# Third transform stage on 64x64 tiles, first stage mostly so, and a new order of all operations

## The chip, the cores and the metric

One Trainium2 chip, of which one core is used. The metric is the device time of one execution in microseconds (us). The engines are called as in the profile: PE (TensorE), PEld (its weight loads), DVE (VectorE), ACT (ScalarE), POOL (GpSimd), SP (SyncE, which here only issues DMAs).

## The reference

Two independent halves over a sequence of 2048 steps and 640 channels, joined along the channels. Half A is a diagonal complex state space model, half B a long convolution by FFT:

```python
Lam_bar = exp(dt * Lam);  B_bar = ((Lam_bar - 1) / Lam)[:, None] * Bmat
h_t = Lam_bar * h_(t-1) + B_bar @ x_t
a = 2 * Re(h @ C.T) + x * Dskip

k_shift = causal 4-tap convolution of k with shift_k      # per channel
kv = k_shift * v
y = irfft(rfft(pad(kv)) * rfft(pad(ssm_k)))[:2048] + kv * ssm_D
b = q * y
out = concat(a, b)                                       # (1, 2048, 1280), bfloat16
```

## The kernel before

The kernel records 815 operations with their footprints in SBUF, and then emits them in an order that stands in the source as a table, `ORDER`: an entry `219T2` is operation 219 on engine T (PE) with its accumulators from PSUM bank 2; A is ACT, V is DVE, G is POOL, S is SP. Each engine runs its entries strictly in the table's order; semaphores between engines follow from the footprints. So the table sets which engine empties which PSUM group, which PSUM banks a group waits for, and the order of the DMAs on SP. A small letter `t` says that a PE operation is issued *narrow*, on smaller tiles of the array.

Half A: `ld_x`, `ld_B` (L512, L517, L547) load, `up2`, `up1`, `up0` (matmuls L581 and L602, evictions L598, L622, L648) build sums over 2, 4, 8 and 16 steps, `coarse` scans over blocks of 16 (`cs_...`, L679 to L690), `dn3` to `dn0` with their additions `ad3` to `ad0` (matmuls L225 and L229, additions L728 on DVE; on ACT, L726, the addition is a second matmul by the identity and a copy) bring the states back down, and the sixteen `C` products (matmuls L225 or L229, eviction `ev_C`, L754) project them, with `xd` (L737, x times D, which waits for `ld_Dr`) added. `gC` (L571, L575) scales the C matrix. The factors come from `dt`, `rn` (Exp on ACT, L383 and L388), `al_s` (Sin, L414), a chain of small DVE steps (`pv`, `dtf`, `rho` ... `fi`), POOL (`fn1`, `ph`) and four expansions `rr` (L457).

Half B, in two halves of 320 channels (0 and 1): the taps of the short convolution, `cm` on ACT (L206) or DVE (L205) and their sums `ca` (L840) and product with v `cx` (L841), per block d of 128 channels; there is one buffer for k, so `ld_k` of block d+1 (L814) waits for the last tap of block d (`cm0_0` for block 1). `pl` writes a finished block to DRAM (L847), the relay `rl` reads it back in another layout (L857). Then the transforms: `s1h`, `s1k` (matmuls L876 wide, L881 narrow, eviction `e1`, L886), `s2` (L900, eviction `e2`, L913), the products `pp`, `pq`, `py`, `pz` (L924 to L931), `r2`, the third stage (L951 wide, L948 narrow, eviction `er2`, L956), `r1` (L972, eviction `er1`, L988 or L990), `em1` (L995), and stores. Tables of sines for these come from POOL (`wqh` L309, `gqh` L350) and ACT (`w_s` L314, `g_s` L354, `i_s` L325, `f1_s` L289), and for the scan `sph` (L472), `sin`, `cos` (L477, L478).

`P.narrow` holds the operations that stand in the table with a small t; in `s1` and `r2` it chooses between two forms.

Of the kernel before, what the change touches and what calls it, by code (L numbers as in the profile page):

```python
# [1097 lines left out]
def plain_order(P):  # L1098
# [16 lines left out]


ORDER = (
# [40 lines left out]
)  # L1158


# [68 lines left out]
```

## Time and profile before

| | us |
|---|---|
| median of 3 runs (188.85 to 190.1) | 190.03 |
| span of the profiled execution | 187.3 |
| busy: PE, PEld | 175.6, 126.3 |
| busy: DVE, ACT, POOL | 158.0, 147.7, 72.6 |

The page gives no time of the profiled execution beside its span; the median lies 2.7 us above it. Granted TensorE clock: 0.999 over the span. Busy time is the union of an engine's instructions; an engine that is idle beside another that sets the pace costs nothing. In the tables by line, `out<-in` are the program's tiles: nearly all lie in one big SBUF buffer, `arena`, and all accumulators in `acc`.

### The profile page before, as it was taken

To read this page: it belongs to the slowest core of one execution; us is meant where nothing else is said; L and a number is where in the kernel's file an instruction comes from. 1 tells how busy PE (TensorE), PEld (TensorE's weight loads), DVE (VectorE), ACT (ScalarE), POOL (GpSimd) and SP (SyncE) were. 2 spreads that over 40 slices of the span, in tenths; PEclk is the share of its full clock that TensorE was granted. 3 is DMA by queue.
4 is the path that set the end of the run, shared out by engine and by line. 5 is a ranking of instruction groups with operands and counts; after the bars stand their busy time and mean duration, and the time that the engine had idled before them with its cause. 6 is when DMAs were issued, how large, how long until landed. Compare 5 with 4: busy or idle time off the path is not lost.

```text
span 187.3 us, 7665 instructions
## 1 busy us (share of the span) xinstructions
PE 175.6 (94%) x3398; PEld 126.3 (67%) x3399; DVE 158.0 (84%) x225; ACT 147.7 (79%) x181; POOL 72.6 (39%) x68
## 2 busy tenths in 40 slices
PE   7998999999799979979997999999999999999992
PEld 2565666677468756656685688776588876887770
DVE  3537964679959899999969999899999999998961
ACT  2469699989899979999997997997898883985000
POOL 8679999900000000008803925730740000551620
PEclk9999999999999999999999999999999999999999
DMA  5999999799999989999989479402496993058996
GB/s 153 191 184 158 200 143 140 141 174 182 198 253 154 290 179 152 180 182 154 138 109 251 154 170 133 75 5 72 122 196 120 210 227 85 15 160 187 208 219 173
DMA packets 106682, 30.15 MB, mean 161 GB/s; under 512 B 101274, under 2 KB 106010, under 8 KB 106650
## 3 DMA queue, kind: packets, MB, share of 16 engines
q1 hardware_dynamic: 106332, 29.35, 86.7%
q8 instruction: 26, 0.43, 1.1%
q10 hardware_dynamic: 318, 0.33, 0.6%
q14 instruction: 6, 0.05, 0.1%
HBM read 11.32 MB, written 7.86 MB: 102 GB/s over the span
## 4 chain that ended last, share of the span: by engine, by line
PE 54%; DVE 23%; DMA 9%; ACT 8%; issue 3%; DVEq 0%; ACTq 0%
PE acc L225 17%; PE acc L581 13%; DMA arena<-in_B_k_dram 9%; PE acc L229 6%; DVE arena L728 6%; PE acc L900 6%; DVE arena L205 5%; ACT arena L913 5%; PE acc L951 4%; DVE arena L840 3%; PE acc L972 3%; PE acc L539 2%; DVE arena L754 2%; PE acc L881 1%; ACT arena L886 1%
## 5 line engine op out<-in xcount | busy, mean ns | idle before, releaser
L581 PE MATMUL acc<-arena 128*64 128x512 bf16 x400 | 45.6, 380 | 1.8 <-DVE arena L457 1.1
L913 ACT CAST arena<-acc 128x960 bf16<-128x960 f32 (+1 forms) x43 | 37.4, 916 | 4.0 <-PE acc L900 2.2
L225 PE MATMUL acc<-arena 128*128 128x320 bf16 (+2 forms) x255 | 36.4, 297 | 2.2 <-DVE arena L754 1.1
L581 PEld LDWEIGHTS <-arena 128*64 128x64 bf16 x400 | 26.0, 110 | 17.8 <-DVE arena L457 1.3
L886 ACT CAST arena<-acc 128x1024 bf16<-128x1024 f32 x37 | 35.8, 1034 | 2.1 <-PE acc L881 2.0
L225 PEld LDWEIGHTS <-arena 128*128 128x128 bf16 x256 | 23.7, 98 | 12.1 <-DVE arena L754 1.3
L841 POOL TENSOR_TENSOR arena<-arena 128x2048 bf16<-128x2048 bf16 x2 | 8.8, 4410 | 53.7 <-DVE arena L840 46.1
L900 PE MATMUL acc<-arena 128*64 128x160 bf16 x512 | 23.6, 235 | 1.8 <-DVE arena L679 1.4
L900 PEld LDWEIGHTS <-arena 128*64 128x64 bf16 x512 | 18.6, 110 | 8.3 <-ACT arena L913 2.2
L229 PE MATMUL acc<-arena 128*64 128x320 bf16 (+3 forms) x258 | 23.2, 313 | 0.5 <-DVE arena L690 0.5
L840 DVE TENSOR_TENSOR arena<-arena 128x2048 bf16<-128x2048 bf16 x14 | 17.6, 1256 | 4.5 <-ACT arena L206 4.3
L728 DVE TENSOR_TENSOR arena<-acc,arena 128x1024 bf16<-128x1024 f32 (+2 forms) x19 | 20.4, 1114 | 0.9 <-PE acc L229 0.5
L760 POOL TENSOR_TENSOR arena<-arena 128x640 bf16<-128x640 f32 x3 | 4.2, 1416 | 32.6 <-ACT arena L752 32.6
L956 ACT CAST arena<-acc 128x1024 bf16<-128x1024 f32 x16 | 15.4, 1025 | 1.7 <-PE acc L951 1.6
L229 PEld LDWEIGHTS <-arena 128*64 128x64 bf16 x258 | 13.0, 110 | 3.5 <-DVE arena L690 0.6
L876 PE MATMUL acc<-arena 128*64 128x128 bf16 x400 | 14.6, 220 | 0.2 <-ACT arena L886 0.2
L876 PEld LDWEIGHTS <-arena 128*64 128x64 bf16 x400 | 12.9, 110 | 2.4 <-ACT arena L886 0.9
L205 DVE TENSOR_SCALAR arena<-arena 128x2048 bf16<-128x2048 bf16 x15 | 11.0, 749 | 3.6 <-DMA arena<-in_B_k_dram 3.5
L754 DVE TENSOR_TENSOR arena<-acc,arena 128x640 bf16<-128x640 f32 x13 | 10.7, 820 | 3.5 <-PE acc L225 2.2
L206 ACT ACTIVATE arena<-arena 128x2048 bf16<-128x2048 bf16 (+2 forms) x10 | 11.1, 1112 | 1.5 <-DMA arena<-in_B_k_dram 1.5
L924 DVE TENSOR_TENSOR arena<-arena 128x2560 bf16<-128x2560 bf16 x8 | 11.9, 1484 | 0.1
L602 PE MATMUL acc<-arena 128*64 128x256 bf16 (+2 forms) x140 | 11.6, 291 | 0.1
(142 smaller groups left out, 284.4 us busy)
## 6 DMA issues: line engine op xcount, KB each, us to landing
out_dram<-arena SPq DMA_DIRECT2D x32, 160.0 KB, 3.3
arena<-in_B_ssm_k_dram SPq DMA_DIRECT2D x8, 320.0 KB, 6.1
kv_rows<-arena SPq DMA_DIRECT2D x5, 512.0 KB, 4.7
arena<-kv_rows SPq DMA_DIRECT2D x16, 160.0 KB, 4.0
arena<-in_A_x_dram SPq DMA_DIRECT2D x16, 160.0 KB, 3.5
arena<-in_B_q_dram SPq DMA_DIRECT2D x8, 320.0 KB, 6.3
arena<-in_A_B_im_dram ACTq DMA_DIRECT2D x1, 160.0 KB, 2.8
arena<-in_A_B_re_dram SPq DMA_DIRECT2D x1, 160.0 KB, 3.0
```

What stands on the lines that cost most here:

```text
L205: vm = lambda e: lambda out, in_, by: e.tensor_scalar_mul(out=out, in0=in_, scalar1=by)
L225: e.matmul(out, lhsT=lhsT, rhs=rhs, start=start, stop=stop, skip_group_check=True)
L229: e.matmul(out[half], lhsT=lhsT[:, half], rhs=rhs, start=start, stop=stop, skip_group_check=True, tile_position=(0, 64 * r))
L581: e.matmul(o[64 * r:64 * r + 64], lhsT=self.BT[j][:, r, d, :], rhs=self.XP[:, d, 2 * q:2 * q + 2], start=(d == 0), stop=(d == 4), skip_gro ...
L728: e.tensor_tensor(out=o, in0=b, in1=o, op=ALU.add)
L754: e.tensor_tensor(out=two(ys), in0=two(B)[:, :, 0:320], in1=two(ys), op=ALU.add)
L840: P.add(f"ca{d}_{j}", tt, lambda e: e.tensor_tensor(out=t1, in0=t1, in1=t2, op=ALU.add), outs=[t1], ins=[t1, t2])
L876: e.matmul(B[64 * b:64 * b + 64, 128 * i:128 * i + 128], lhsT=lh[i], rhs=F[:, b, :], start=True, stop=True, tile_position=(0, 64 * b))
L886: P.add(f"e1{what}{hf}_{u}", {PACT: act(1024), PDVE: dve(1024)}, lambda e, B: c.CP[e](out=out, in_=(B.rearrange("p (l n s k) -> p k s l n" ...
L900: e.matmul(B[64 * s:64 * s + 64, 512 * b + 160 * i:512 * b + 160 * i + 160], lhsT=c.W[:, k, 64 * b:64 * b + 64], rhs=self.AS[hf][:, k, 160 ...
L913: c.CP[e](out=out, in_=b.rearrange("p r (k j n) -> p r k j n", k=n, j=4) if nj > 1 else b.rearrange("p r (k x) -> p r k x", k=n))
L956: P.add(f"er2{hf}_{u}", {PACT: act(1024), PDVE: dve(1024)}, lambda e, B: c.CP[e](out=out, in_=B.rearrange("p (s n b) -> p b s n", s=2, n=4 ...
```

## The change

Only the table `ORDER` differs. It issues 18 of the 20 `r2` operations narrow (before: none) and 34 of the 40 `s1` operations (before: 15), moves about 70 evictions and small operations between engines, and puts all operations in a new order. POOL runs 65 instead of 64 operations. Two of the 46 old and 44 new lines of the table:

```diff
-    "168A0 156G0 161S0 0V0 58G0 6T0 17G0 167A0 162S0 110G0 19V0 147G0 87V0 11G0 18V0 89A0 90S0 12G0 3T1 42G0 13V0 88S0 182S0 "
+    "0V0 161A0 30G0 167S0 7T0 26G0 17G0 168A0 162S0 58G0 20V0 110G0 21V0 122V0 112G0 8T1 19V0 87V0 46G0 125V0 23V0 89A0 28V0 36V0 "
...
-    "557T2 564A4 684T0 789G0 558V2 559V0 678T6 685A0 680T4 679V6 783G0 790S0 690T2 681A4 682T0 691V2 686T6 556G0 784S0 683A0 "
+    "787T0 672V0 780V0 673V0 782A4 777V0 783G0 557T2 788A0 778S0 688t6 558V2 686t4 689A6 694t0 565G0 687V4 559G0 692t2 695A0 560T6 "
```

In a narrow `s1` each of eight groups is 4 matmuls of 64x64 by 64 columns, which leave out the zero half of a block diagonal factor, instead of 2 matmuls of 128x64 by 128 columns. In a narrow `r2` each 64x128 by 128 matmul is two of 64x64.

What the new table does on single engines, at three places. First ACT at the start of the program, ahead of its first evictions of `up2` (L598); `js0` is L206 128x64, `f1_s` L289, `dt` L383, the copies of the turned B matrix L526. Before:

```order
L383 ACT_TABLE_LOAD
L383 ACTIVATE arena<-arena 128x10
L526 COPY arena<-acc 128x640 x3
L388 ACTIVATE arena<-arena 128x10 x3
L526 COPY arena<-acc 128x640
L598 CAST arena<-acc 128x2x2x256
L388 ACTIVATE arena<-arena 128x10 x2
L414 ACT_TABLE_LOAD
L414 ACTIVATE arena<-arena 128x80
```

And now, at the same place:

```order
L206 ACT_TABLE_LOAD
L206 ACTIVATE arena<-arena 128x64
L289 ACT_TABLE_LOAD
L289 ACTIVATE arena<-arena 128x64
L383 ACT_TABLE_LOAD
L383 ACTIVATE arena<-arena 128x10
L388 ACTIVATE arena<-arena 128x10
L526 COPY arena<-acc 128x640 x2
L388 ACTIVATE arena<-arena 128x10
L526 COPY arena<-acc 128x640
L388 ACTIVATE arena<-arena 128x10
L354 ACT_TABLE_LOAD
```

`js0` and `f1_s` moved ahead of `dt`, one `rn` moved ahead of the first copies, and three loads of the activation table stand where there was one.

Second, the stretch that follows on ACT, now up to the first tap of block 0 (L206 128x2048) and `sin` (L477); `rn` is L388, `al_s` L414, `sw` L796:

```order
L796 CAST arena<-arena 128x20
L388 ACT_TABLE_LOAD
L388 ACTIVATE arena<-arena 128x10
L414 ACT_TABLE_LOAD
L414 ACTIVATE arena<-arena 128x80
L598 CAST arena<-acc 128x2x2x256
L354 ACTIVATE arena<-arena 128x32x32 x2
L388 ACT_TABLE_LOAD
L388 ACTIVATE arena<-arena 128x10
L598 CAST arena<-acc 128x2x2x256
L314 ACT_TABLE_LOAD
L314 ACTIVATE arena<-arena 128x1024
```

Two of the five `rn` moved in among the sines, each with a load ahead of it and one behind it; before, nothing but the load ahead of `al_s` stood there.

Third, DVE after the scan's last step (L690), up to the additions of the level below. Before:

```order
L690 TENSOR_TENSOR arena<-arena 128x5x128
L840 TENSOR_TENSOR arena<-arena 128x2048
L728 TENSOR_TENSOR arena<-acc,arena 128x5x128
L886 CAST arena<-acc 128x64x2x8
L728 TENSOR_TENSOR arena<-acc,arena 128x4x256
L728 TENSOR_TENSOR arena<-acc,arena 128x256 x2
L575 CAST arena<-acc 128x2x320
L205 TENSOR_SCALAR arena<-arena 128x2048 x2
L728 TENSOR_TENSOR arena<-acc,arena 128x4x256
L728 TENSOR_TENSOR arena<-acc,arena 128x2x2x256 x2
L913 CAST arena<-acc 128x2x3x160
L205 TENSOR_SCALAR arena<-arena 128x2048
```

And now:

```order
L690 TENSOR_TENSOR arena<-arena 128x5x128
L728 TENSOR_TENSOR arena<-acc,arena 128x4x256
L728 TENSOR_TENSOR arena<-acc,arena 128x5x128
L886 CAST arena<-acc 128x64x2x8 x2
L728 TENSOR_TENSOR arena<-acc,arena 128x256
L205 TENSOR_SCALAR arena<-arena 128x2048
L728 TENSOR_TENSOR arena<-acc,arena 128x256
L205 TENSOR_SCALAR arena<-arena 128x2048
L728 TENSOR_TENSOR arena<-acc,arena 128x4x256
L913 CAST arena<-acc 128x2x3x160 x2
L728 TENSOR_TENSOR arena<-acc,arena 128x2x2x256
L205 TENSOR_SCALAR arena<-arena 128x2048
```

The evictions of gC (L575) and one of the two 1024-wide additions left DVE for ACT; one more e1k (L886) and one more e2k (L913) came.

74 rows, old and new, of the table ORDER are left out of this document.

## The prediction

> **What bounds the kernel now.** First the page: three engines are nearly full, and the average does not say which of them sets the end.
>
> ```profile
> PE 175.6 (94%) x3398; PEld 126.3 (67%) x3399; DVE 158.0 (84%) x225; ACT 147.7 (79%) x181; POOL 72.6 (39%) x68
> ```
>
> So I cut the span at DVE instructions that I know by name: the landing of the second k block (41.15), of the fourth (65.20), `ev_C0` (98.5), `ev_C4` (127.9), `er10_16` (161.8) and the last eviction (184.4). The view of busy time by stretch then reads (length, PE, PEld, DVE, ACT, POOL):
>
> ```profile
> 41.15:65.20 24.05, 22.81 (x373) 16.52 (x369) 21.18 (x27) 22.60 (x34) 0.00 (x0) 1.00 1.12 214
> 65.20:98.50 33.30, 29.98 (x743) 21.56 (x740) 31.48 (x41) 31.78 (x40) 8.14 (x2) 1.00 1.05 157
> 98.50:127.90 29.40, 28.15 (x650) 21.38 (x653) 28.11 (x29) 26.27 (x30) 15.30 (x6) 1.00 0.59 125
> 127.90:161.80 33.90, 33.29 (x791) 25.31 (x781) 32.79 (x41) 27.33 (x33) 5.62 (x4) 1.00 0.73 143
> 161.80:184.40 22.60, 21.80 (x516) 17.08 (x514) 18.96 (x22) 8.34 (x9) 9.50 (x6) 1.00 0.74 181
> ```
>
> DVE idles 2.9, 1.8, 1.3 and 1.1 us in the first four, out of 120.7. From the landing of k1 to 161.8 DVE is the bound, and ACT beside it up to 98.5. PE's 90 to 98% hides its own waits, because the modelled ends of matmuls overlap. Only the last stretch, four C products and the end of r1, is PE's: DVE idles 3.6 us there. Where DVE does idle before that, the timeline names transposing loads:
>
> ```profile
> 41.15 1.42 DVE L205 TENSOR_SCALAR arena<-arena 128x2048 bf16<-128x2048 bf16 x2 [0.90 <-DMA arena<-in_B_k_dram]
> 53.96 0.75 DVE L205 TENSOR_SCALAR arena<-arena 128x2048 bf16<-128x2048 bf16 x1 [1.90 <-DMA arena<-in_B_k_dram]
> 65.20 1.42 DVE L205 TENSOR_SCALAR arena<-arena 128x2048 bf16<-128x2048 bf16 x2 [0.65 <-DMA arena<-in_B_k_dram]
> 97.87 0.49 DVE L737 TENSOR_TENSOR arena<-arena 128x640 bf16<-128x640 bf16 x1 [1.38 <-DMA arena<-in_A_Dskip_dram]
> ```
>
> Thus the time is: when k1 lands, plus DVE's work from there, plus DVE's waits, plus PE's tail.
>
> **PE's part of the change, costed at nothing.** The rows of a wide s1, a narrow s1, r1, a wide r2, and a change of tile shape:
>
> ```profile
> 122.93 1.55 PE L876 MATMUL acc<-arena 128*64 128x128 bf16 x48 [0.16 <-ACT arena L886]
> 97.40 1.00 PE L881 MATMUL acc<-arena 64*64 64x64 bf16 x96
> 153.27 1.63 PE L972 MATMUL acc<-arena 64*64 64x80 bf16 x160
> 161.65 5.50 PE L951 MATMUL acc<-arena 64*128 64x128 bf16 x160
> 108.20 0.61 PE L900 MATMUL acc<-arena 128*64 128x160 bf16 x12
> 108.73 0.75 PE L881 MATMUL acc<-arena 64*64 64x64 bf16 x64
> 112.39 2.79 PE acc L900 x72
> 105.64 0.62 PE L229 MATMUL acc<-arena 128*64 128x512 bf16 x4
> 106.10 0.61 PE L876 MATMUL acc<-arena 128*64 128x128 bf16 x16
> ```
>
> A wide s1 takes 1.55/3 = 0.52 us, a narrow one 1.00/3 = 0.33; narrow goes from 15 to 34 operations: -19 x 0.19 = -3.6 us. No trace row shows a narrow r2 (32 matmuls on 64x64 tiles, 128 columns). By r1, 10.2 ns for 80 columns, it is 16.3 ns per matmul and 0.52 us, against 5.50/10 = 0.55 wide. If r1's pace held whatever the width, it would be 0.33; if splitting in two doubled it, 1.1. I take 0.52, the nearest row: -18 x 0.03 = -0.5. Changes of tile shape rise from 52 to 65; the twelve matmuls at 108.20 hold PE 0.53 us ahead of one, against 2.79/6 = 0.46 in a row (the chain's 72): 13 x 0.07 = +0.9. Three more additions on ACT (`ad1_0`, `ad1_6`, `ad0_9`; `ad3_0` leaves) double their matmuls by identity ones, 0.46 each from 105.64 to 106.10, less 0.3: +1.0. Net: -2.2 us. DVE covers it: in the r2 stage ACT and DVE empty PSUM at one operation per 1/(1/1.025 + 1/1.218) = 0.56 us, which is already the 0.55 that PE shows.
>
> ```profile
> L956 ACT CAST arena<-acc 128x1024 bf16<-128x1024 f32 x16 | 15.4, 1025 | 1.7 <-PE acc L951 1.6
> L956 DVE CAST arena<-acc 128x1024 bf16<-128x1024 f32 x4 | 4.7, 1218 | 0.0
> ```
>
> Without that cover a narrow r2 at 1.1 would lengthen r2 by 18 x 0.55 = 10 us; the s1 rows speak against that, since there the split made an operation shorter, so I exclude it and keep up to +1.5.
>
> **Term 1, k1 lands later: +3.7 us.** The new order mixes Exp and Sin on ACT, and so the program has eight table loads where it had two.
>
> ```profile
> 2.29 1.28 ACT L383 ACT_TABLE_LOAD   x1 [2.29 <-DVE arena L258]
> 6.56 0.21 ACT L383 ACTIVATE arena<-arena 128x10 bf16<-128x10 f32 x1 [3.00 <-DVE arena L378]
> 7.92 1.29 ACT L526 COPY arena<-acc 128x640 bf16<-128x640 bf16 x2 [0.56 <-PE acc L524]
> 12.82 1.28 ACT L414 ACT_TABLE_LOAD   x1
> 14.11 0.27 ACT L414 ACTIVATE arena<-arena 128x80 f32<-128x80 int32 x1
> 30.30 2.00 ACT L206 ACTIVATE arena<-arena 128x2048 bf16<-128x2048 bf16 x1
> 10.38 0.22 POOL L406 COPY arena<-arena 128x10 int32<-128x10 int32 x1 [2.68 <-DVE arena L300]
> 12.83 0.32 POOL L410 TENSOR_TENSOR arena<-arena 128x80 int32<-128x80 int32 x1
> 8.25 0.16 DVE L385 TENSOR_TENSOR arena<-arena 128x10 f32<-128x10 f32 x1
> 29.80 5.08 SPq L814 DMA_TRANSPOSE arena<-in_B_v_dram  x1
> 34.99 2.69 SPq L814 DMA_TRANSPOSE arena<-in_B_k_dram  x1
> ```
>
> Now: the load before `dt` sits behind `js0` and `f1_s`, which wait for DVE and have loads of their own; I estimate `dt` at 7.2 instead of 6.56. `rn` waits for `rho` (8.25 + 0.65), and both `ev_B0` now stand behind it: done at 10.4 instead of 9.2 at the latest (the copies at 7.92 end), so PE's first `up2` starts about 1.2 us later, which also hides that `ld_sk` and `ld_D` now stand ahead of three x loads on SP. `fn1` on POOL comes at 11.0, `ph` ends 5.0 us of POOL work later at 16.0 (13.15 now). ACT needs a load for `g_s` (which waits for `gqh`, 13.3), one for `rn`, one for `al_s`: 13.3 + 1.13 + 0.35 + 1.28 + 0.2 + 1.28 + 0.27 = 17.8 against 14.38. From there to the end of `cm0_0` stand 17.9 us of work in the new order (four taps at 2.0, three evictions at 1.0, three `g_s` at 1.15, three `w_s` at 1.06, `sin` 1.27, the rest 1.0; starts overlap by 0.1 each) and two more loads, 2.6: 38.3, or 39 if `sin` waits for `sph` on POOL. Now it ends at 32.30, and `ld_k1`, which overwrites the only k buffer, is issued at 34.99 because `ld_v0` held SP. Then it is issued at 38.7: +3.7. At the low end ACT's 7.3 idle us before 14 swallow all but the two late loads, and k1 is 0.5 late; at the high end POOL's waits make it 5.
>
> [...]
>
> **Term 2, DVE from k1 to k3's taps: +0.7.** There `cx0`, `e1h0_0`, `ev_up21_4`, three up0 evictions and the first two steps of the coarse scan enter (8.2 us), two `rr`, `gm` and small ones leave (4.9). The 3.3 us first fill the waits of 1.90 and 0.65.
>
> **Term 3, DVE from k3's taps to `ev_C0`: -3.4.**
>
> ```profile
> L886 DVE CAST arena<-acc 128x1024 bf16<-128x1024 f32 x3 | 3.6, 1215 | 0.0
> L913 DVE CAST arena<-acc 128x960 bf16<-128x960 f32 x3 | 3.5, 1154 | 0.0
> L575 DVE CAST arena<-acc 128x640 bf16<-128x640 f32 x4 | 3.3, 815 | 0.0
> L728 DVE TENSOR_TENSOR arena<-acc,arena 128x1024 bf16<-128x1024 f32 x16 | 18.8, 1217 | 0.9 <-PE acc L229 0.5
> ```
>
> Four gC evictions leave (3.3), with `e1k0_1`, `ad1_0`, `e2k0_8` (3.6), `xd0`, an up0b eviction and the two scan steps (2.2): 9.1. `ad3_0`, two e1k and two e2k enter (5.6).
>
> **Term 4, the wait for D: -1.4.** `xd0` goes to POOL and `ld_Dr` stands ahead of `ld_v3` and `ld_k4` on SP instead of behind them and the four loads of h1.
>
> **Term 5, ACT and the relay behind it: +1.8.** SP now issues a `ld_C1` ahead of `pl2`, and another inside the relay:
>
> ```profile
> 70.90 1.79 SPq L556 DMA_TRANSPOSE arena<-in_A_C_im_dram  x1
> 78.98 1.03 ACT L886 CAST arena<-acc 128x1024 bf16<-128x1024 f32 x1
> 96.80 2.04 ACT L206 ACTIVATE arena<-arena 128x2048 bf16<-128x2048 bf16 x1
> ```
>
> So the first half of the relay is complete 3.4 us later than k1's shift alone says, at about 81, which leaves PE's first s1k at 81.3 (77.1 now, with 3 us of slack), and its eviction at 82 (78.98). From there to `cm4_0` ACT has 20 instructions of 17 us, as now (17.8): the last of s2k is out at 97.6, `C0` ends at 99.8, `ev_C0` runs at 99.9. By terms 1 to 4 alone DVE would be there at 98.1: +1.8. The bounds are 0 (the relay lands in time) and 3.5.
>
> **Term 6, DVE after that: +0.2.** To `er10_16` DVE's instructions sum to 64.7 us instead of 64.4 by their rows; `xd1` (0.5) leaves right behind `ev_C0`, the rest grows. **Term 7, the tail: +0.4.** One r1 of 0.43 us moves behind `r10_16`; the last C products stay PE-bound.
>
> Sum: 3.7 + 0.7 - 3.4 - 1.4 + 1.8 + 0.2 + 0.4 = +2.0 us. The profiled span of 187.3 becomes 189.3; the median of the runs, 190.03, lies 2.7 above the span, so **192.0**.
>
> **Rivals.** *PE was the bound after all, or ACT hides its loads* (0.2); the page's chain speaks for it:
>
> ```profile
> PE 54%; DVE 23%; DMA 9%; ACT 8%; issue 3%; DVEq 0%; ACTq 0%
> ```
>
>  In this case terms 1 and 5 are near zero and 0.7 - 3.4 - 1.4 + 0.2 + 0.4 = -3.5 remains: 186.5. It decides where `cm0_0` still ends before 35, when `ld_v0` leaves SP. *The delay is absorbed* (0.2): ACT catches up before C0, term 5 is 0: 190.2. *The whole delay arrives* (0.15): PE's s1k waits for the relay and DVE runs dry there, so term 3 saves nothing: 195.4. The forecast itself has 0.45, from 190.5 to 194.
>
> The range takes the terms' bounds: 186 to 196. One per cent, about what a measurement of this kernel can tell from no change, is 1.9 us. Faster holds the first rival, 0.2; slower the third and 0.6 of the forecast, 0.42; within 0.38.
>
> **What would show it.** Eight table loads of 1.28 us; `ld_k1` on SP near 38.7 and k1's taps on DVE near 44.9; no wait of DVE for D; s1k's first eviction near 82; `ev_C0` near 99.9; r21's ten operations still at 0.55 us each; s1 narrow at 0.33. I am wrong if k1 lands before 42, or if DVE is no longer full between 65 and 160.

## The result, and the profile after

The changed kernel takes **207.5 us** (median of 4, 206.76 to 208.19) against 189.4 for the kernel before on the same chip: ratio 1.099, 95% interval 1.091 to 1.108. The forecast was 192.0 with a range of 186 to 196, so the sign was right and the time was missed by 15.5 us. Losses below are given as ratios to the kernel before, measured beside each run; the ratios leave out slow executions, more than 1.5% above the fastest of their kernel, which the medians keep. 1% is 1.9 us.

The page of the changed kernel, with the lines that answer to the one shown of before and two more: the clock that TensorE was granted (all nines before), and the queue `q8` of instructions, whose packets are compared with TensorE's program further below.

```profile
PE 187.8 (91%) x4066; PEld 132.7 (65%) x4066; DVE 162.4 (79%) x229; ACT 151.2 (74%) x181; POOL 75.1 (37%) x69
...
PEclk9999999799999999975999999999999999999999
...
q8 instruction: 32, 0.52, 1.2%
```

Every engine is busier in us and less busy as a share, and the clock has two dips, near 36 and near 92 us. TensorE has 668 more matmuls; before, `q8` had carried

```profile
q8 instruction: 26, 0.43, 1.1%
```

That is six packets more; the prediction does not count them. Here is the span of the changed kernel cut at the same instructions (first tap of k1, first tap of k3, `ev_C0`, `ev_C4`, `er10_16`, last eviction), in the columns of the prediction:

```profile
43.66:70.50 26.84, 26.84 (x580) 18.56 (x580) 24.87 (x31) 23.62 (x34) 2.33 (x1) 1.00 1.11 197
70.50:106.48 35.98, 30.00 (x695) 19.93 (x691) 31.31 (x35) 30.06 (x41) 10.91 (x4) 0.91 1.09 173
106.48:140.02 33.54, 32.27 (x900) 23.38 (x902) 31.56 (x33) 29.36 (x31) 14.86 (x6) 1.00 0.60 115
140.02:173.46 33.44, 33.00 (x772) 26.61 (x770) 29.16 (x35) 23.05 (x28) 9.16 (x5) 1.00 0.56 108
173.46:202.46 29.00, 27.24 (x784) 23.34 (x784) 18.56 (x23) 7.81 (x9) 4.00 (x3) 1.00 0.59 147
```

The stretches were 24.05, 33.30, 29.40, 33.90 and 22.60 us long. So 2.5 us are lost before k1's taps, then 2.8, 2.7, 3.7 in the next two together (`ev_C4` now runs 2.8 us behind the end of its product, so the cut between them has moved), and 6.4 in the tail. DVE, called the bound, idles 4.7 us in the second row and 4.3 us in the fourth; it no longer decides there. Three places hold most of the loss.

**The table loads.** Eight, 1.28 us each; from the timeline of ACT (start, us, line):

```profile
2.62 1.28 ACT L206 ACT_TABLE_LOAD   x1 [2.62 <-DVE arena L263]
...
14.10 1.28 ACT L388 ACT_TABLE_LOAD   x1
15.62 1.28 ACT L414 ACT_TABLE_LOAD   x1
20.38 1.28 ACT L388 ACT_TABLE_LOAD   x1
22.80 1.28 ACT L314 ACT_TABLE_LOAD   x1
```

```profile
38.65 2.30 SPq L814 DMA_TRANSPOSE arena<-in_B_k_dram  x1
```

`ld_k1` is issued at 38.65, where the prediction had 38.7. Behind these loads an eviction of `up2` on ACT comes late, and TensorE waits for it once, up to 35.27; the clock is halved from 35.44 for 3.4 us, which is the dip near 36. From the waits, and busy time with the clock (third from the end):

```profile
PE acc L581 <- ACT arena L598: 2.2, 1, 2.2
35.00:40.00 5.00, 4.72 (x28) 2.18 (x30) 5.00 (x5) 4.38 (x5) 2.48 (x2) 0.66 0.40 85
```

**A stop of TensorE up to 91.87, and half the clock from within it.** Busy time in stretches of 5 us, the two rows in question, and from the timeline the row that begins when the stop ends, with ACT's next row:

```profile
85.00:90.00 5.00, 2.83 (x135) 2.18 (x128) 4.97 (x6) 4.08 (x6) 3.28 (x2) 1.00 1.04 210
90.00:95.00 5.00, 3.13 (x74) 1.74 (x73) 2.25 (x4) 1.36 (x2) 2.17 (x1) 0.51 1.09 139
```

```profile
91.87 0.64 PE L881 MATMUL acc<-arena 64*64 64x64 bf16 x32 [2.37 <-issue]
...
94.40 1.01 ACT L726 CAST arena<-acc 128x1024 bf16<-128x1024 f32 x1 [3.64 <-PE acc L229]
```

"Issue" says that TensorE waited for nothing that the profile shows. The granted clock is 0.51 from 90 to 95 us (halved from 90.05 for 6.8 us), and ACT and DVE run dry there (1.36 and 2.25 us busy of 5). `ev_C0` comes at 106.48 instead of the 99.9 forecast.

**A third stage of twice the length.** The groups of r2's lines, narrow (L948) and its evictions on ACT:

```profile
L956 ACT CAST arena<-acc 128x1024 bf16<-128x1024 f32 x17 | 16.7, 1019 | 8.5 <-PE acc L948 8.4
L948 PE MATMUL acc<-arena 64*64 64x128 bf16 x576 | 18.7, 282 | 0.2 <-issue 0.2
L948 PEld LDWEIGHTS <-arena 64*64 64x64 bf16 x576 | 17.9, 213 | 0.8 <-issue 0.6
```

A narrow r2 starts 0.96 to 1.01 us after the one before it, where the two stand in a row and no stop lies between, and a wide one takes 0.55; and ACT idles 8.4 us waiting for it (1.6 before).

### The profile page after: what moved, and what is told of

Read it like the earlier page. It is cut to its first block, busy times and chain, and to the rows that moved or that the text cites. A ratio compares the mean times of both kernels' runs of the same rounds, so it can differ in the third digit from the quotient of the medians.

```text
span 205.5 us, 8999 instructions
## 1 busy us (share of the span) xinstructions
PE 187.8 (91%) x4066; PEld 132.7 (65%) x4066; DVE 162.4 (79%) x229; ACT 151.2 (74%) x181; POOL 75.1 (37%) x69
## 4 chain that ended last, share of the span: by engine, by line
PE 59%; ACT 20%; DVE 11%; POOL 4%; issue 4%; ACTq 0%; DVEq 0%; POOLq 0%
PE acc L229 14%; PE acc L225 12%; PE acc L581 11%; PE acc L948 9%; ACT arena L913 5%; DVE arena L728 5%; PE acc L881 4%; PE acc L900 4%; PE acc L602 3%; ACT arena L206 3%; ACT arena L575 2%; PE acc L972 2%; POOL arena L350 2%; DVE arena L754 1%; DVE arena L886 1%
## 5 line engine op out<-in xcount | busy, mean ns | idle before, releaser
L581 PEld LDWEIGHTS <-arena 128*64 128x64 bf16 x400 | 24.6, 113 | 22.6 <-ACT arena L598 2.7
L886 ACT CAST arena<-acc 128x1024 bf16<-128x1024 f32 x36 | 35.0, 1034 | 4.0 <-PE acc L881 2.9
L913 ACT CAST arena<-acc 128x960 bf16<-128x960 f32 (+1 forms) x39 | 34.1, 904 | 5.1 <-PE acc L900 2.9
L229 PE MATMUL acc<-arena 128*64 128x320 bf16 (+3 forms) x406 | 34.6, 320 | 0.5
L225 PE MATMUL acc<-arena 128*128 128x320 bf16 (+3 forms) x183 | 27.7, 302 | 2.1 <-DVE arena L690 1.4
L229 PEld LDWEIGHTS <-arena 128*64 128x64 bf16 x406 | 22.1, 113 | 7.5 <-issue 1.4
L225 PEld LDWEIGHTS <-arena 128*128 128x128 bf16 x183 | 16.6, 98 | 9.4 <-ACT arena L886 2.1
L900 PEld LDWEIGHTS <-arena 128*64 128x64 bf16 x512 | 19.0, 110 | 4.5 <-ACT arena L913 2.5
L948 PE MATMUL acc<-arena 64*64 64x128 bf16 x576 | 18.7, 282 | 0.2 <-issue 0.2
L737 POOL TENSOR_TENSOR arena<-arena 128x640 bf16<-128x640 bf16 x5 | 7.0, 1397 | 31.7 <-DMA arena<-in_A_Dskip_dram 29.9
L948 PEld LDWEIGHTS <-arena 64*64 64x64 bf16 x576 | 17.9, 213 | 0.8 <-issue 0.6
L881 PEld LDWEIGHTS <-arena 64*64 64x64 bf16 x1088 | 11.4, 110 | 10.0 <-issue 6.6
L881 PE MATMUL acc<-arena 64*64 64x64 bf16 x1088 | 13.9, 197 | 3.4 <-issue 2.9
L598 DVE CAST arena<-acc 128x1024 bf16<-128x1024 f32 x7 | 8.5, 1219 | 7.3 <-ACT arena L414 6.1
L205 DVE TENSOR_SCALAR arena<-arena 128x2048 bf16<-128x2048 bf16 (+1 forms) x16 | 12.2, 773 | 1.5 <-DMA arena<-in_B_k_dram 1.3
```

Of the source, the lines that this page charges most:

```text
L225: e.matmul(out, lhsT=lhsT, rhs=rhs, start=start, stop=stop, skip_group_check=True)
L229: e.matmul(out[half], lhsT=lhsT[:, half], rhs=rhs, start=start, stop=stop, skip_group_check=True, tile_position=(0, 64 * r))
L581: e.matmul(o[64 * r:64 * r + 64], lhsT=self.BT[j][:, r, d, :], rhs=self.XP[:, d, 2 * q:2 * q + 2], start=(d == 0), stop=(d == 4), skip_gro ...
L881: e.matmul(B[64 * b:64 * b + 64, 512 * l + 64 * i:512 * l + 64 * i + 64], lhsT=lh[i][ps], rhs=F[ps, b, 64 * l:64 * l + 64], start=True, st ...
L886: P.add(f"e1{what}{hf}_{u}", {PACT: act(1024), PDVE: dve(1024)}, lambda e, B: c.CP[e](out=out, in_=(B.rearrange("p (l n s k) -> p k s l n" ...
L900: e.matmul(B[64 * s:64 * s + 64, 512 * b + 160 * i:512 * b + 160 * i + 160], lhsT=c.W[:, k, 64 * b:64 * b + 64], rhs=self.AS[hf][:, k, 160 ...
```

## The experiments

In `ORDER` an entry is a number, an engine letter and a bank; a small `t` makes an operation narrow.

### The third stage

Wide again in the changed kernel (e1), and narrow in the kernel before (e2):

```diff
- ... 678t0 ... 696t2 ... 680t6 ...      (18 entries)
+ ... 678T0 ... 696T2 ... 680T6 ...
```

> The changed kernel with the tile split of the third stage (r2) taken back in its 18 operations; order and everything else as changed. Theory A (a narrow r2 costs 1.0 us of TensorE against 0.5 wide, because each of its 32 pairs of weight load and matmul takes as long as one of the 16 wide pairs): the r21 stage from r10_16 to C8 shrinks from 11.3 to 6 us, the eight narrow r20 operations save up to another 4, total 197 to 202 us. Rival B (the pace of r2 is set by ScalarE's evictions or by the new order): r2 operations stay near 1.0 us apart, total 205 to 208.

> The kernel before with the 18 r2 operations of the change as 64x64 tiles and nothing else changed. Theory A: 1.0 us an operation, 9 us more at most, 195 to 199 us. Rival B: 189 to 191 us.

Measured: e1 200.7 us, ratio 1.062 (1.048 to 1.076) instead of 1.099; e2 197.6 us, ratio 1.050 (1.041 to 1.059). Theory A holds: the tile split of r2 costs 5% by itself and 3.7% within the change, and rival B is out. It does not say why a pair of load and matmul takes 30 ns. Weights of a wide and of a narrow r2 are columns of Y that lie 80 bytes apart, so e7, in the kernel before, takes them from a matrix whose elements stand side by side (the third stage's output is then left out):

```diff
-  e.matmul(B[ms, ...], lhsT=lh[i][s][r][:, ms], rhs=rh, ...)
+  e.matmul(B[ms, ...], lhsT=c.W[64 * s:64 * s + 64, 2 * i + r, ms], rhs=rh, ...)
```

> The kernel before with the 18 r2 operations as 64x64 tiles, but with their weights read from the constant matrix W, 64 elements side by side, in place of columns of Y that lie 80 bytes apart; so the third stage's output is left out. Theory H (the weight load of a narrow tile is slow because its columns lie apart): r2 at 0.3 to 0.6 us an operation, weight load near 110 ns, total 187 to 191 us. Rival I (a 64x64 tile with 128 moving columns takes 30 ns a pair whatever its weights): 0.95 to 1.0 us an operation, total 195 to 199 us.

The weight loads of e2, the groups of e7, and two rows of e7's timeline in the r21 stage:

```profile
L948 PEld LDWEIGHTS <-arena 64*64 64x64 bf16 x576 | 17.7, 212 | 0.8 <-ACT arena L752 0.3 <-issue 0.3
```

```profile
L948 PE MATMUL acc<-arena 64*64 64x128 bf16 x576 | 10.1, 218 | 4.0 <-issue 4.0
L948 PEld LDWEIGHTS <-arena 64*64 64x64 bf16 x576 | 8.6, 107 | 5.3 <-issue 4.9
```

```profile
164.67 1.98 PE L948 MATMUL acc<-arena 64*64 64x128 bf16 x128 [1.15 <-issue]
168.40 0.92 PE L948 MATMUL acc<-arena 64*64 64x128 bf16 x51 [1.74 <-issue]
```

The weight load falls from 212 ns in e2 to 107, and operations start 0.44 to 0.57 us apart where no stop lies between: theory H for the pace. (e7 changes the tensor that the weights come from together with their spacing.) The total, 192.9 us in one run, is above H's 187 to 191; TensorE now stops for 4.0 us of "issue" in these operations. The faster narrow operations run into stops of the kind that is taken up below.

### Table loads, and the order without narrow operations

e3 brings two `rn` forward and puts `f1_s` and `js0` behind the last `rn` on ACT; two loads are left:

```diff
- 15A0 (js0) ... 34A0 (f1_s) ... 94A0 ... 98A0 ... 99A0 ... 100A0 ... 97A0 ... 101A0
+ 94A0 ... 98A0 ... 99A0 ... 100A0 97A0 101A0 34A0 15A0
```

> The changed kernel with four small operations of ScalarE's prologue moved (two rn brought forward, f1_s and js0 put behind the last rn), so that its exponentials stand together and two table loads of 1.28 us are left of eight. Theory C (the delay of 4 us to VectorE's chain arrives at the end): k1's load issued near 35, C0 ended 4 us earlier, total 202 to 204 us. Rival D (the delay is swallowed by the stall of TensorE between 85 and 100 us, which has a cause of its own, the last part of the relay): total 205.5 to 208 us.

> The changed kernel with the changed order kept, but the third stage wide in all 20 operations and the first stage narrow only in the 15 operations that are narrow before. Theory F (TensorE's program arrives in packets of 256 instructions, one packet ahead; narrow operations use them up twice as fast, and TensorE stands still when a packet is late): the stall of 2.4 us ahead of s1k0_9 and the half clock after it go, total 193 to 197 us against 200.7 with 34 narrow. Rival G (the stall is the wait for the relay's last part, whatever the tiles): stall and half clock stay, total 199 to 202 us.

> As e5_order_only, and the four small ScalarE operations moved so that two table loads are left of eight. Theory C (the delay of VectorE's chain arrives): 3 to 4 us less than e5_order_only, 190 to 193 us. Rival D (swallowed): within 1 us of e5_order_only.

e3: ratio 1.080 (1.067 to 1.094), 204.6 us by the median and 202.5 by the ratio: theory C's 202 to 204 and not D's 205.5 to 208. `ld_k1` comes at 36.92, not near 35, and the stop ahead of `s1k0_9` grows to 3.16 us. e5: 198.8 us, ratio 1.060 (1.053 to 1.067). Its stop at 91.87 and the half clock there are gone, as theory F has it, but the total misses F's 193 to 197: it has another stop of 1.56 us at `s1h1_6`, and lies nearer to G's 199 to 202. Against e1 (1.062) the 19 narrow operations of s1 thus cost nothing that can be told in this order. e6: 194.7 us, ratio 1.036 (1.028 to 1.045): the six loads cost 4.1 us against e5, and nearly all of it arrives, from `cm0_0` (37.20 to 33.30) to the last C product (4.4 us). Theory C, where no larger stop hides it. Its 190 to 193 was 2 us too low with e5's. A part of the 4.1 us is not the loads' own time: e5 has half the clock from 34.9 for 3.4 us, after a wait of 2.5 us for ACT, and e6 has neither. In the changed kernel twenty matmuls take 4.04 us at that place, in e12 (below), which has all eight loads but no half clock there, 2.35.

e11 asks for the start of the order, where `ev_B0` waits on ACT behind the first `rn`:

```diff
- 98A0 (rn) ... 166A0 ... 164A5 (the two ev_B0)
+ 166A0 ... 164A5 98A0
```

> As e6_order_two_loads (changed order, narrow set of before, two table loads), and the first rn put behind the two ev_B0 that it stood ahead of on ScalarE. Theory K (the order's own cost begins with up2, which starts 1.8 us later because ev_B0 waits behind rn for VectorE's rho): ev_B0 ends near 8.8 us, up2 starts 1.3 us or more earlier, and 1 to 1.5 us of it arrives: 193 to 194 us against 194.7. Rival L (it is absorbed, since ScalarE's evictions and not TensorE's start set the pace): 194.2 to 195.2 us.

194.5 us, ratio 1.037 (1.026 to 1.048). `ev_B0` ends at 8.16 instead of 10.40, and `up20_4` still starts at 19.66 (19.42 in e6), because it then waits 0.94 us for a load of B. So the traces show rival L, absorbed; the interval alone would not tell 1 us.

### TensorE's program

s1 narrow in the kernel before, in the 34 operations of the change (with two that were narrow already and are not among them, 36):

```diff
- ... 201T4 ... 195T6 ... 191T2 ... 203T0 ...      (21 entries)
+ ... 201t4 ... 195t6 ... 191t2 ... 203t0 ...
```

> The kernel before with the first stage narrow in the 34 operations of the change (15 before) and nothing else changed. If TensorE's time there is hidden by the evictions, as the prediction has it: 188.5 to 190 us. If it counts: 19 operations by 0.2 to 0.25 us, 185 to 187 us.

Both were wrong: 194.1 us, ratio 1.035 (1.027 to 1.043), **slower**, although each narrow s1 does run in 0.27 us. Its page has 336 more matmuls and TensorE stops five times for 0.5 to 1.7 us of "issue".

What these stops have in common is their place in the program. The trace's DMA records have queue `q8` in packets of 16,384 bytes (32 in the changed kernel; 32 times 256 are 8,192, and TensorE has 8,170 records). Here are TensorE's records (weight loads, matmuls, semaphore waits) counted up to each stop over 0.5 us that waits for nothing shown:

```
kernel   operation, stop in us, records ahead of it, modulo 256
after    s1k0_9 2.37: 194    r11_6 0.73: 194
e1       s1k0_9 2.37: 192    r10_28 0.87: 193    r11_22 2.08: 192
e2       C14 1.34: 194
e4       s1k0_8 0.90: 193    s2k0_0 0.54: 194    s1k1_5 0.88: 193    r21_6 0.68: 193    r11_16 1.68: 194
e5       s1h1_6 1.56: 195    C10 0.80: 194
e7       r20_1 0.68: 195     r10_0 0.96: 195     r21_2 1.15: 194     r21_5 1.74: 194    C14 1.13: 195
```

All lie between 192 and 195 of 256, as do 17 more in e3, e6, e8 to e12, e15 and e18; some traces lack one or two records, which moves the count. `q8` has 29 packets in e4, with 672 instructions more than before, and 27 in e17 (below), with 256 more, against 26 before. So a packet is read here as 256 instructions of TensorE. A packet begins when TensorE has about entered the one ahead of it (median lag 1.0 us after, 1.1 before, at most 4.4 and 3.4), takes 0.9 to 1.8 us, and TensorE, where it stood, goes on some 1.2 to 1.7 us after its end (for `s1k0_9` the packet ends at 90.39 and TensorE goes on at 91.87). So by estimate a packet's worth of instructions that is used up in less than about 3.8 us makes TensorE stand, where the next packet has the usual lag; it is no fixed bound, for in the changed kernel four packets used up in 3.3 to 3.6 us (up to 52.3, 113.8, 130.4 and 133.8) brought no stop over 0.3 us. The packet for `s1k0_9` began 4.36 us after that point. Theory F: a narrow operation has twice the instructions of a wide one (64 against 32 in s1 and r2, weight loads included), and where it is also quick (s1: 0.27 us against 0.52) it runs the program dry.

To test it, e8 and e9 add 64 matmuls (128 instructions) to the warm-up in about the same time, so that all boundaries fall half a packet further on (e8 in the operations shown, e9 in `warm` 5, 2, 3 and 8):

```diff
-            for _ in range(2):
-                e.matmul(B[:, 0:512], ...)
+            n, w = (18, 56) if k in (6, 7, 0, 1) else (2, 512)
+            for _ in range(n):
+                e.matmul(B[:, 0:w], ...)
```

> The changed kernel with 64 more matmuls, so 128 more instructions, in the warm-up: four of its operations do 18 matmuls of 56 columns in place of 2 of 512, about the same time. Every later instruction then stands half a packet further on. Theory F (packets of 256): every stop of TensorE that waits for nothing shown again begins at the same count within a packet (192 of 256), so at other operations than before: no stop of 2.4 us ahead of s1k0_9, one of 1 to 3 us two narrow operations earlier if that packet is as late. Rival G (relay): the stop stays ahead of s1k0_9. The total is not what tells them apart: 203 to 209 us.

> The kernel before with 64 more matmuls in the warm-up, as in e8_shift_packets (128 more instructions in about the same time), nothing else. Theory F (packets of 256 instructions, a stop when one is late): the boundaries fall half a packet further on, at operations where they did not fall before; if the kernel before owes its time to boundaries that fall well, stops of 0.5 to 2 us appear at a count of 192 within a packet and the total is 189 to 193 us. Rival J (packets hardly matter where first and third stage are mostly wide): no stop, total within 1 us of the kernel before.

e8 (206.1 us in one run): no stop ahead of `s1k0_9`, and one of 1.60 us ahead of `s1k0_8`, two operations later rather than earlier, as far into its packet (194). Rival G, the relay, is out. e9 is the run that matters: with the work of the kernel before unchanged, 194.2 us, **ratio 1.033 (1.023 to 1.043)**. Its timeline has stops that the kernel before has not (records modulo 256: 193, 192, 193):

```profile
156.34 0.58 PE L973 MATMUL acc<-arena 64*64 64x80 bf16 x42 [1.42 <-issue]
166.52 2.82 PE L952 MATMUL acc<-arena 64*128 64x128 bf16 x83 [0.52 <-issue]
176.03 0.61 PE L973 MATMUL acc<-arena 64*64 64x80 bf16 x23 [2.36 <-issue]
```

> The kernel before with 112 more matmuls in the warm-up, 224 more instructions: almost a whole packet, so the boundaries fall nearly where they fell. Theory F, from the profile of before: packets used up in under 3.8 us cost 5.4 us at 128 more instructions (measured 6.3) and 1.4 us at 224: 188.5 to 190.5 us. Rival N (the extra matmuls themselves cost the time of e9_before_shift): more of them, 195 us or above.

> The kernel before with 128 more matmuls in the warm-up, 256 more instructions: one whole packet, so from the warm-up on every boundary falls where it fell. Theory F: no stop, the time of the kernel before, 187 to 189.5 us (one packet more to fetch, early, where nothing waits). Rival N (the extra matmuls cost the time): 194 us or above.

These add 112 and 128 matmuls in the same way. e15: ratio 1.013 (1.006 to 1.019), 190 us as F had it. e17, exactly one packet: **ratio 1.003 (0.998 to 1.008)**, and the longest wait of this kind in its list of waits is 0.4 us:

```profile
PE acc L882 <- issue: 0.4, 1, 0.4
```

Half a packet costs 6.3 us, seven eighths 2.4, a whole one nothing. Rivals J and N are out: it is the place of the boundaries, and the kernel before has them where they cost nothing.

The same in the changed kernel (32 more instructions), in its order with two loads (208 more), and in the kernel before with s1 wide, as it is and with 220 more:

> The changed kernel with 16 more matmuls, 32 more instructions, in the warm-up. Theory F, from its profile: packets used up in under 3.8 us cost 5.1 us as it stands and 1.4 us at 32 more: 203 to 205 us. Rival J: 206.5 to 208.5 us.

> As e6_order_two_loads (changed order, narrow set of before, two table loads) with 104 more matmuls, 208 more instructions, in the warm-up. Theory F, from the profile of e6: packets used up in under 3.8 us cost 2.9 us as it stands and 0.5 us with the boundaries 208 further on: 191 to 192.5 us; what is left against the kernel before is the order's own. Rival J: 194 to 195.5 us.

> The kernel before with the first stage wide in all 40 operations, so 15 of them go from 0.27 to 0.52 us of TensorE and 480 instructions go. Theory F: two packets fewer, no stops, but up to 15 x 0.25 = 3.7 us more of TensorE, of which evictions hide a part: 187 to 191 us. If narrow operations of the first stage pay for themselves in the kernel before: 190 to 192 us; if their packets cost as much as they save: 187 to 189 us.

> The kernel before with the first stage wide (e10_before_s1_wide) and 110 more matmuls in the warm-up (13 of 78 columns in each of its ten operations in place of 2 of 512): 220 more instructions. Theory F, worked out from the profile of e10: with the boundaries of the packets 220 instructions further on no packet is used up in less than 3.8 us, so the stop of 2.3 us ahead of C10 and the half clock after it go; e10 was 2.4 us ahead of the kernel before until C9, total 185 to 187 us. Rival J (boundaries don't decide; e10's stop is of another kind): 191 to 193 us.

e16: 204.0 us, ratio 1.087 (1.082 to 1.092), within F's 203 to 205: 1.2% less by the ratios for 32 instructions more. Its stop in s1k is gone, but the clock is still halved from 89.94 for 3.4 us (6.8 in the changed kernel), after TensorE waited 1.46 us for DVE up to 88.10; e8 has the same from 90.37. e14: 193.1 us, ratio 1.029 (1.024 to 1.034); no stop is left, yet half a microsecond above F's range. e10: 192.0 us, ratio 1.024 (1.017 to 1.032), above F's 187 to 191, which had no stop; it was 2.3 us ahead of the kernel before at C9 and lost it and more at one boundary:

```profile
155.77 6.47 PE L225 MATMUL acc<-arena 128*128 128x320 bf16 x34 [2.30 <-issue]
```

e13 takes that stop away and comes to 189.9 us, ratio 1.012 (1.007 to 1.017): better than e10, but its 2.3 us ahead are gone (a wait of 2.05 us of `s2h0_27` for DVE, which e10 has not, ends at 67.97), so 185 to 187 was wrong and it does not beat the kernel before.

Why a packet begins late: e12 leaves out two transposing loads.

```diff
+  None if f"{n}{d}" in ("v3", "k4") else e.dma_start_transpose(...)
```

> The changed kernel with two transposing loads left out (ld_v3 and ld_k4, issued between 81 and 88 us), so that the taps of the fourth and fifth block work on old data. Theory F (the packet for s1k0_9 is late, 4.4 us from its request to its beginning, because the core's DMA queues are full of these transfers): the packet begins within 2 us of its request, the stop ahead of s1k0_9 is below 0.5 us and the clock stays at full speed from 90 to 97 us. Rival M (the packet is late for a reason in TensorE's own sequencer): the stop stays above 1.5 us. The total also gains from the waits that the two loads took with them, so it is not what tells them apart.

205.2 us in one run. The packet for `s1k0_9` begins 2.04 us after TensorE went on into the packet ahead of it, 3.88 in the changed kernel. But TensorE had just stood 1.47 us at that boundary (0.29 in the changed kernel), because the packet ahead began later (2.8 us behind its own point against 1.3); from the beginning of that stop it is 3.5 against 4.2 us. The stop ahead of `s1k0_9` is still 2.06 us, M's number (here the view puts it down to DVE, L886), and the clock is still halved, from 91.77 for 3.4 us. So this run does not show that other transfers make the packets late; what sets the lag is open.

Last, the changed kernel with its causes taken away together: r2 wide, two loads, 108 more instructions.

> The changed kernel with the third stage wide, two table loads (as e3_two_loads) and 54 more matmuls, 108 more instructions, in the warm-up; the order and the 34 narrow operations of the first stage are kept. From e1's profile packets used up in under 3.8 us cost 5.4 us there and 1.0 us with boundaries 112 further on. Theory F: 200.7 - 4.1 (loads) - 2 to 4.4 = 192 to 194.5 us. Rival J (the place of the boundaries doesn't matter with 34 narrow operations): 196 to 197.5 us.

198.4 us, ratio 1.060 (1.052 to 1.068): a miss by 4 us, and above J's 196 to 197.5 too. It has stops of 1.71 us in s1k, 2.72 right behind it (ahead of `dn2_4`) and 2.67 in r11, where the packets began 3.1, 3.9 and 5.2 us after TensorE reached the one ahead; a fixed 3.8 us does not foretell them. With 34 narrow operations and two loads, neither of the two places of the boundaries that were run (e3, e18) is free of long stops there.

## Why the prediction was wrong, step by step

- **PE's part, costed at nothing: the step that failed.** The narrow r2 was taken as 0.52 us by r1's pace. It takes 0.96 to 1.01. The bound of 1.1 stood in the text with its price, 10 us, and was excluded because the split had made s1 shorter. But s1 narrow halves its columns as well as its tile (64 against 128), and r1 and s1 have weights side by side; r2 keeps 128 columns for twice the matmuls and reads its weights 80 bytes apart. By e7, where the weights stand side by side, the same tiles and columns take 0.45, and with e2's weights 0.96. Cost: 6.8 us in the change, 10.2 alone. Nor did the evictions cover it: ACT idled 8.4 us.
- **What the sum did not have at all: the instructions.** I counted TensorE's time and not its program. 668 more matmuls bring six more packets, and the boundaries move. The prediction's "-3.6 us" for s1 was right by duration (0.27 us) and came out as nothing (e5 to e1) or as +6.5 us (e4).
- **Term 1 was right.** Eight loads of 1.28 us; `ld_k1` at 38.65 (38.7 forecast, +3.66 against +3.7); 4.1 us at the end by e5 and e6. `al_s` starts at 16.92, 0.02 us after the load at 15.62 has ended (0.01 before: 14.10 and 14.11), so such a load cost its 1.28 us and no more there.
- **Terms 2 and 4.** k3's taps came 5.3 us later against 4.4 forecast, and DVE has no wait for D any more. **Terms 3 and 5.** The first eviction of s1k came at 82.54 (82 forecast). Then `ev_C0` was to follow at 99.9 and came at 106.48: about 3.2 us go with the stop and the half clock (e5, without them and with fewer narrow operations, has 103.24), and for another 3.3 no stop accounts. DVE's 3.4 us saved do not arrive: it idles 4.7 us in this row, and the prediction called it the bound up to there.
- **Term 7.** From the start of C8 to the end of the last C product 17.6 us against 16.5, with 0.73 us of it a stop.
- **"I am wrong if k1 lands before 42, or if DVE is no longer full between 65 and 160."** k1's first tap runs at 43.66 (44.9 forecast); DVE is not full. The rival "the whole delay arrives" (195.4) came nearest, in part by luck: the loads' delay does arrive (e5 to e6), but the long stop in s1k is not a wait for the relay (e8), and the narrow r2 and the packets are not in it.

By the ratios, the change's 9.9% are 3.7 for the narrow r2, 2.4 for the loads, about 0.2 for s1, and 3.6 for the order with its boundaries, of which moving them (e14) takes 0.7 back. By the intervals each of these differences is uncertain by 1 to 1.6%, and they hold for this order of taking back alone: with two loads, 34 narrow s1 instead of 15 make 2.4% (e18 against e6, with boundaries at other places). The remaining 2.9%, 5.4 us, is not settled. In e14's profile the last C product ends at 185.74 instead of 183.60, and the span goes on for 6.1 us behind it instead of 3.7, where SP still issues stores; TensorE has three more additions by identity matmuls. That these are the causes is argued, not shown.

## What to carry to other kernels

Count instructions as well as time: here the split into smaller tiles doubled the instructions of an operation (668 matmuls and six packets more in all), and short operations in a row used a packet up before the next one was there (stops of 2.37 us in the first stage and 0.73 in r1). Before explaining a change of 3%, shift the program by some warm-up instructions and by one whole packet: if the time goes and returns (here +3.3% with 128 instructions and +0.3% with 256), the difference is the place and not the work. And a bound that only an analogy excludes stays in the range; look at whether the analogous row has the same columns and the same weights' stride (here 0.45 us side by side and 0.96 at 80 bytes).

## What the runs showed of the hardware

- The 8,170 TensorE records of the changed kernel went with 32 packets of 16,384 bytes on `q8`, the 6,834 of the kernel before with 26; a packet began a median of 1.0 and 1.1 us after TensorE had about entered the one ahead. Stops over 0.5 us that wait for nothing shown lie at one count modulo 256 (192 to 195), and 128 instructions in the warm-up cost the kernel before 3.3% (e9), 256 nothing that can be told (e17: ratio 0.998 to 1.008).
- A weight load of a 64x64 tile took 107 ns with elements side by side (e7) and 212 with elements 80 bytes apart (e2); the operation 0.45 and 0.96 us.
- In these cases the clock was halved for 3.4 or 6.8 us from within a stretch in which TensorE stood or up to 1.8 us behind it: the changed kernel from 90.1 for 6.8 (stop of 2.37) and from 35.4 for 3.4 (wait of 2.2 for ACT), e10 from 156.7 for 3.4 (2.30), e9 from 175.8 for 3.4 (2.36), e16 from 89.94 for 3.4 (wait of 1.46 for DVE). Not each such stretch did it: e18's stop of 2.67 in r11 and e12's wait of 2.08 us for ACT, up to 35.27, brought none, and what decides is open.
